# Top-k attention and a routed MoE on one core: one scores tile of two PSUM banks for each head, transposed tails beside the scores of a later unit, and the first q and k pairs loaded in the order of the rest

## The chip, the cores and the metric

One Trainium2 chip, one core of it. The metric is the device time of one launch in microseconds (us); a run of the kernel before takes 391.32 us in the median of three.

## What is computed

Attention over 2 batches, 8 heads, 576 positions of 64 columns, in which each query keeps its 32 largest scores; its rows (1152 tokens of 512 columns) go through a top-1 router to 8 experts of 512 x 1024 x 512.

```python
scores = scale * np.matmul(q, k.transpose(0, 1, 3, 2))
kth = np.partition(scores, -32, axis=-1)[..., -32:-31]
scores = np.where(scores >= kth, scores, -1e9)
attn = np.exp(scores - scores.max(-1, keepdims=True)); attn /= attn.sum(-1, keepdims=True) + 1e-9
x = np.matmul(attn, v)                     # -> (1152, 512)
expert = argmax(x @ w_gate); h = np.maximum(disp @ w1, 0); y = h @ w2
out[i] = gate[i] * y[expert[i], pos[i]]
```

## The kernel before, in words

**Units and rounds.** Queries come in 9 tiles of 128 rows, heads in 4 pairs: 36 units `u` of 128 queries and two heads. `attention` (L1028) writes the program out round by round; round `i` works on several units at once, each at another step. In a round's order: `penalty` of unit i-3 (L391), `heads` of unit i (L289), `sign_turn` of unit i-1 (L363), `shift` of unit i (L339), `probs` of unit i-3 (L400), half of `values` of unit i-4 (L424), `scores` of unit i+1 (L272), the other half of `values`, two steps of `select` for unit i-2, `merge` of unit i (L303). Each engine executes its own instructions in the order in which they are written; the framework adds the semaphore waits between engines, tile by tile. `LAG` and the tables `side`, `early`, `late`, `mid`, `act`, `pool`, `end` say in which round the routing of tokens, the loads and splits of weights and the first expert's matmuls are issued.

**One unit.** PE writes the scores of both heads (L281, eight matmuls, sixteen where a tile spans both batches). VectorE (DVE) takes the 8 largest of each 64-column segment straight from PSUM (`MAX8`, L296, 18 of them, with small steps of earlier units filled in between). ScalarE (ACT) copies the rest: `nn` (L340), then `sm`, the scores less their maximum, one instruction for each head (L343), which are the last reads of the scores in PSUM. Then the sign and its count on ACT (L353), a product on GpSimd (POOL, L360), two 576-column `MAX8` on DVE (L384), the small `nk` (L388), and the penalty on ACT (L398). `probs` transposes `sm` and adds the transposed penalty on PE (L415, L416), four blocks of 128 columns for each head, and ACT takes the exponential (L417). The last 64 columns of both heads, the **tail**, go together as a ninth block: transposed in a tile of its own, `pTt` (L406, L407), exponential in L408. `values` multiplies with v (L437, L440).

**PSUM, 8 banks.** `pD` 1, `pV` 1, `pT` 2 (a tile of each in turn), `pTt` 1, and `trio` 3: in attention these three are one tile `pS` in which head 0 has columns 0 to 575 and head 1 columns 576 to 1151; before and after attention they are three single banks, `TAIL_P`.

**The start.** q and k of batch 0 are loaded pair by pair (`load_qk`, L86), split into two 16-bit halves (`split_qk`), transposed on PE (L231, L234) into PSUM and copied to `qk` in SBUF (`take`, L236; L241 on ACT, L243 on DVE). Pairs 0 and 1 are loaded so that a partition holds 6 consecutive positions, 1536 bytes in one piece; after the transpose the copy puts position 6t+r at its place, writing every sixth element. Pairs 2 and 3 are loaded with 96 positions apart, in pieces of 256 bytes, and the copy is straight. Round 0 starts when the copies of pair 0 are done; pair 1 is copied by ACT before `shift` of unit 0. `swap_q` (L207) makes, by DMA, a copy of q with its halves exchanged. `warm` (L1022) issues matmuls whose result nobody reads.

**Small users of `pTt`.** `pick`, `pick_row`, `check`, `count` and `warm(few)` put a small matmul's result there (L933, L960, L979, L996, L1023).

Of the kernel before, what the change touches and what calls it, by code (L numbers as in the profile page):

```python
# [34 lines left out]
def kernel(  # L35
# [35 lines left out]
    def trio(one):  # L71
        if TRIO.get("one") != one:
            trio_end()
            TRIO["one"], TRIO["cm"] = one, tc.tile_pool(name=f"pS{one}", bufs=1, space=bass.MemoryType.PSUM)
            TRIO["pool"] = TRIO["cm"].__enter__()
        if one:
            return TRIO["pool"].tile([128, 3, 512], FT, name="pS", bufs=1)
        return [TRIO["pool"].tile([128, 512], FT, name=f"pS{i}", bufs=1) for i in range(3)]

# [6 lines left out]
    def load_qk(b, p, tag="nat", names="qk"):  # L86
        for name in names:
            src = q if name == "q" else k
            XN[name, b, p] = x = work.tile([PR, 2, R, D], FT, name=name + "nat", tag=tag, bufs=4 if tag == "nat" else 2)
            for j in range(2):  # L90
                nc.sync.dma_start(x[:, j], bass.AP(
                    tensor=src.tensor, offset=src.offset + (b * H + 2 * p + j) * S * D,
                    ap=[[D, PR], [PR * D, R], [1, D]] if b or p > 1 else [[R * D, PR], [D, R], [1, D]]))

# [141 lines left out]
    def take(p, slot, j, pt, eng):  # L236
        o, pt = qk_of(0)[slot][:, 2 * p + j], pt[:, :S]
        if p < 2:
            o, pt = o.rearrange("p (t r) -> p r t", r=R), pt.rearrange("p (r t) -> p r t", r=R)
        if eng is nc.scalar:  # L240
            eng.activation(o, pt, AF.Copy)  # L241
        else:
            eng.tensor_copy(o, pt)  # L243
# [28 lines left out]
    def scores(u):  # L272
        t, p = divmod(u, HP)

        PS[u] = trio(1).rearrange("p g c -> p (g c)")
        for j in range(2):
            h = 2 * p + j
            for c0, c1 in ((0, 512), (512, S)) if j == 0 else ((0, 1024 - S), (1024 - S, S)):
                for row, n, b, s in parts(t):
                    for i in range(2):  # L280
                        nc.tensor.matmul(PS[u][row:row + n, j * S + c0:j * S + c1], QK[b][2 * i][:, h, s:s + n],  # L281
                                         QK[b][1][:, h, c0:c1], start=(i == 0), stop=(i == 1))

    def scores_of(u, j):
        return PS[u][:, j * S:(j + 1) * S]

# [112 lines left out]

    def probs(u, j):  # L400
        sm = SM[u].rearrange("p j s -> p (j s)")
        pen = PEN[u].rearrange("p j s -> p (j s)")
        if j == 2:
            PTT[u] = work.tile([128, 128], FT, name="pTt")
            pt = psum.tile([128, 128], FT, name="pTt", bufs=1)
            nc.tensor.matmul(pt, sm[:, 512:640], ident, start=True, stop=False, is_transpose=True)  # L406
            nc.tensor.matmul(pt, pen[:, 512:640], identb, start=False, stop=True)  # L407
            nc.scalar.activation(PTT[u], pt, AF.Exp, scale=-scale)  # L408
            return
# [520 lines left out]
    def pick(e, step):  # L930
        if step == 0:
            PK[e] = (psum.tile([128, 128], FT, name="pTt", bufs=1), CG[:, e])
        pc, g = PK[e] if e < 2 else (PKR[1][0], CG[:, 3])  # L933
# [24 lines left out]
    def pick_row(e, step):  # L958
        if step == 0:
            PKR[e] = (psum.tile([128, 128], FT, name="pTt", bufs=1), CG[:, 2 * e])  # L960
            nc.tensor.matmul(PKR[e][0][:1, :E], onesb[:, 0:1], OHS, start=True, stop=True)
# [15 lines left out]
    def check(step):  # L977
        if step == 1:
            pf = psum.tile([128, 128], FT, name="pTt", bufs=1)  # L979
            nc.tensor.matmul(pf[:1, 0:1], onesb[:, 0:1], fl[:, 0:1], start=True, stop=True)  # L980
# [14 lines left out]
    def count():  # L995
        pc = psum.tile([128, 128], FT, name="pTt", bufs=1)  # L996
        nc.tensor.matmul(pc[:1, :E], onesb[:, 0:1], OHS, start=True, stop=True)
# [24 lines left out]
    def warm(n, few=False):  # L1022
        o = psum.tile([128, 128], FT, name="pTt", bufs=1) if few else TAIL_P[2]  # L1023
        x = onesb if few else onesb[:, None, :].to_broadcast([128, 4, 128])
# [3 lines left out]
    def attention(side, early, late, mid, act, pool, end):  # L1028
        nc.vector.memset(OHS, 0.0)
        def run(fs):  # L1030
            for f, *a in fs:
                f(*a)
# [3 lines left out]
        for i in range(NU - 1):  # L1036
# [27 lines left out]
            last = i == NU - 2  # L1064
            exps = at(3, probs, 0) + at(3, probs, 1) + at(3, probs, 2)
            run(exps + at(0, shift) if last else at(0, shift) + exps)
            run(routes((1, 1.5)))
            half, nxt = at(4, values, 1), at(-1, scores)
            run(at(4, values, 0) + (half + nxt if last else nxt + half) + routes((0, 3, 3.5)))
            run(mid.get(i, []) + at(2, select, 1) + at(2, select, 2))  # L1070
# [146 lines left out]
    split_qk(0, 1, 0, POOL, DVE, 2)  # L1217
    pt = [psum.tile([128, 1024], HF, name=f, bufs=n) for f, n in (("pT", 2), ("pT", 2), ("pTt", 1))]
    pt += [a.bitcast(HF) for a in TAIL_P[:2]] + [pv.bitcast(HF)]
    for i, j, sw, o, eng in ((0, 0, 0, 0, ACT), (0, 1, 0, 1, ACT), (0, 0, 2, 3, DVE), (1, 0, 0, 4, ACT),  # L1220
# [137 lines left out]
```

## Time and profile before

| | |
|---|---|
| median of 3 runs | 391.32 us (389.61 to 392.37) |
| profiled execution: its time | 391.26 us |
| its span, first to last instruction | 389.5 us |
| DVE busy | 325.0 us (83%) |
| PE busy | 329.7 us (85%) |
| ACT busy | 303.2 us (78%) |
| POOL busy | 273.9 us (70%) |

The span is what the profile resolves; 1.8 us of the profiled execution's time lie around it. The program has a start (to about 40 us), 36 rounds of some 6.2 us, their end (to about 285 us), and the remaining experts. Busy shares are means over these stages. A PE matmul's length is modelled, and PE's clock has two levels, 1.2 and 2.4 GHz; the profile shows the granted one as 0.50 and 1.00. Line numbers are those of the kernel before; in the changed kernel L281 is L277, L296 is L292, L340 and L343 are L336 and L339, L241 is L237, and L398 is L394, while L406 to L440 keep their numbers.

### The profile page before, as it was taken

The numbers are of one execution on the slowest core, as the hardware profiler recorded it, in microseconds if no ns is written. First come the engines' busy times: TensorE is split into PE (matmuls) and PEld (weight loads), VectorE is DVE, ScalarE is ACT, GpSimd is POOL, SyncE is SP. The second block draws the span as 40 slices with busy tenths as digits, with TensorE's granted clock in tenths as the row PEclk, the third lists the DMA queues.
The fourth block names the chain that finished last, engine by engine and source line by source line (L and its number), as shares of the span: only waits on it lengthen the run. The fifth ranks groups of instructions, "written<-read, shape, count | busy, mean of one in ns | idle before, by whom it ended". The sixth has DMA issues, their size and how long they took to land.

```text
span 389.5 us, 10253 instructions
## 1 busy us (share of the span) xinstructions
PE 329.7 (85%) x3387; PEld 276.0 (71%) x3390; DVE 325.0 (83%) x1863; ACT 303.2 (78%) x573; POOL 273.9 (70%) x293
## 2 busy tenths in 40 slices
PE   5556588789889887978898999999989999899791
PEld 2245477677768776867677888999746996897681
DVE  5747999998998999999999998989791669969920
ACT  6978899998898899989897999796553767768610
POOL 4366595889695678998977989976631459579541
PEclk9556999996997999999988999999999999999997
DMA  8132989794738150304032302557459999999210
GB/s 191 25 91 57 200 199 222 203 236 91 108 65 270 40 206 31 109 3 136 2 109 57 110 2 66 138 164 265 186 102 383 314 317 350 331 333 372 56 31 24
DMA packets 66085, 60.28 MB, mean 155 GB/s; under 512 B 47461, under 2 KB 48229, under 8 KB 66023
## 3 DMA queue, kind: packets, MB, share of 16 engines
q1 hardware_dynamic: 63879, 54.79, 51.3%
q0 software_dynamic: 1616, 4.73, 3.3%
q8 instruction: 28, 0.46, 0.5%
q14 instruction: 34, 0.28, 0.2%
q10 hardware_dynamic: 528, 0.02, 0.1%
HBM read 40.66 MB, written 12.09 MB: 135 GB/s over the span
## 4 chain that ended last, share of the span: by engine, by line
PE 47%; DVE 36%; ACT 10%; issue 3%; DMA 2%; SPq 0%; POOL 0%; ACTq 0%; POOLq 0%
DVE un L296 14%; PE pS L281 7%; PE pV L440 7%; DVE z L384 6%; PE pS L656 6%; PE pT L656 5%; ACT qk L241 4%; PE pT L415 4%; PE pT L738 3%; DVE ws L618 3%; PE pV L656 2%; PE pD L656 2%; PE pT L416 2%; ACT ws L612 2%; DVE wk L319 1%
## 5 line engine op out<-in xcount | busy, mean ns | idle before, releaser
L296 DVE MAX8 un<-pS 128x8 f32<-128x64 f32 x648 | 110.4, 219 | 14.8 <-PE pS L281 14.0
L360 POOL TENSOR_TENSOR z<-sm,sg 128x576 f32<-128x576 f32 x71 | 89.6, 1280 | 21.3 <-ACT sg L353 21.0
L618 POOL TENSOR_TENSOR ws<-wr,ws 128x1024 bf16<-128x1024 f32 x29 | 66.5, 2298 | 18.2 <-ACT ws L612 17.2
L440 PE MATMUL pV<-vm,pT 128*128 128x65 f32 (+1 forms) x640 | 76.9, 270 | 0.0
L281 PE MATMUL pS<-qk 128*128 128x512 f16 (+7 forms) x320 | 47.9, 311 | 33.2 <-DVE na L313 15.5
L656 PEld LDWEIGHTS <-ws 128*128 128x128 f16 (+1 forms) x1056 | 70.3, 98 | 6.6 <-issue 4.7
L440 PEld LDWEIGHTS pV<-vm,pT 128*128 128x128 f32 (+1 forms) x640 | 73.2, 188 | 0.8
L281 PEld LDWEIGHTS <-qk 128*128 128x128 f16 (+1 forms) x320 | 26.3, 109 | 54.5 <-issue 39.2
L618 DVE TENSOR_TENSOR ws<-wr,ws 128x1024 bf16<-128x1024 f32 x35 | 60.7, 1766 | 2.7 <-ACT ws L612 2.2
L415 PE MATMUL pT<-ident,sm 128*128 128x128 f32 x288 | 58.5, 292 | 0.5 <-ACT xT L505 0.5
L353 ACT ACTIVATE sg<-sm,mx 128x576 bf16<-128x576 f32 x72 | 55.0, 767 | 3.2 <-DVE mx L336 2.8
L398 ACT ACTIVATE pen<-sm,nk 128x576 bf16<-128x576 f32 x70 | 50.7, 773 | 6.7 <-DVE nk L388 6.5
L416 PE MATMUL pT<-identb,pen 128*128 128x128 bf16 x288 | 54.7, 227 | 1.0 <-ACT pen L398 0.9
L384 DVE MAX8 z<-z 128x8 f32<-128x576 f32 x72 | 50.8, 747 | 0.0
L612 ACT ACTIVATE ws<-wr 128x1024 f16<-128x1024 f32 x50 | 49.8, 1047 | 0.1
L343 ACT ACTIVATE sm<-pS,mx 128x576 f32<-128x576 f32 x72 | 49.3, 736 | 0.6 <-issue 0.3
L415 PEld LDWEIGHTS pT<-ident,sm 128*128 128x128 f32 x288 | 43.0, 149 | 5.7 <-ACT xT L505 1.6
L417 ACT ACTIVATE pT<-pT 128x512 f32<-128x512 f32 x72 | 39.4, 600 | 2.7 <-PE pT L416 2.5
L661 POOL DMA_INDIRECT out_dram<-y,xp x12 | 17.5, 1462 | 27.7 <-ACT y L803 14.0
L416 PEld LDWEIGHTS <-pen 128*128 128x128 bf16 x288 | 31.1, 109 | 2.1 <-ACT pen L398 1.9
L656 PE MATMUL pS<-xe,ws 128*128 128x128 f16 (+7 forms) x312 | 22.0, 227 | 0.6 <-DVE ws L618 0.6
L542 POOL DMA_INDIRECT xbuf<-xs,ru x9 | 10.1, 1118 | 16.5 <-DVE xs L537 6.5
(257 smaller groups left out, 652.1 us busy)
## 6 DMA issues: line engine op xcount, KB each, us to landing
wr<-in_moe_w_dram SPq DMA_DIRECT2D x32, 1024.0 KB, 6.0
xbuf<-zero SPq DMA_DIRECT2D x6, 771.0 KB, 6.1
qnat<-in_q_dram SPq DMA_DIRECT2D x16, 144.0 KB, 3.5
knat<-in_k_dram SPq DMA_DIRECT2D x16, 144.0 KB, 3.5
out_dram<-zero SPq DMA_DIRECT2D x3, 768.0 KB, 4.6
vm<-in_v_dram SPq DMA_DIRECT2D x16, 128.0 KB, 3.0
qk<-qk SPq DMA_DIRECT2D x14, 144.0 KB, 2.5
vt<-in_v_dram SPq DMA_DIRECT2D x4, 64.0 KB, 3.2
```

What stands on the lines that cost most here:

```text
L281: nc.tensor.matmul(PS[u][row:row + n, j * S + c0:j * S + c1], QK[b][2 * i][:, h, s:s + n], QK[b][1][:, h, c0:c1], start=(i == 0), stop=(i ...
L296: nc.vector.max(out=un[:, j, i], in_=scores_of(u, j)[:, i * w:(i + 1) * w])
L353: nc.scalar.activation(SG[u][j], SM[u][:, j], AF.Sign, bias=VAL[u][0][:, 2, j:j + 1], scale=-(1.0 - 2.0 ** -20), accum_out=CNT[:, c:c + 1])
L360: engs[j].tensor_tensor(out=Z[u][:, j], in0=SM[u][:, j], in1=SG[u][j], op=OP.mult)
L384: nc.vector.max(out=z8[:, step - 1], in_=Z[u][:, step - 1])
L398: nc.scalar.activation(PEN[u][:, j], SM[u][:, j], AF.Relu, bias=NK[u][:, j:j + 1], scale=BIG)
L415: nc.tensor.matmul(pt[:, c], sm[:, o:o + 128], ident, start=True, stop=False, is_transpose=True)
L416: nc.tensor.matmul(pt[:, c], pen[:, o:o + 128], identb, start=False, stop=True)
L440: nc.tensor.matmul(PV[t][row:row + n, h0 + half], PT[u][:, half, c, row:row + n], VM[b][:, c, p, half], start=False, stop=(half == 1 and c ...
L612: nc.scalar.activation(h[:, d], r[:, s], AF.Copy)
L618: eng.tensor_tensor(out=l[:, d], in0=r[:, s], in1=h[:, d], op=OP.subtract)
L656: nc.tensor.matmul(o, a(i), c(i), start=(i == 0 and m == 0), stop=(i == k - 1 and m == 2))
```

## The change

Head 0 and head 1 of a unit get a tile of two banks each (`pS0`, `pS1`), four banks in all; the fourth is that of `pTt`, which is gone. The transposed tail of unit i-3 is written into columns 640 to 767 of head 1's tile of unit i+1, after that unit's scores and before the second half of `values`. For the last four units it takes a fourth single bank or, for unit 32, a tile `pT`. The small users of `pTt` take a tile `pT`. Pairs 0 and 1 of q and k of batch 0 are loaded as the others are, and their copies are straight.

```diff
         if one:
-            return TRIO["pool"].tile([128, 3, 512], FT, name="pS", bufs=1)
-        return [TRIO["pool"].tile([128, 512], FT, name=f"pS{i}", bufs=1) for i in range(3)]
+        return [TRIO["pool"].tile([128, 1024 if one else 512], FT, name=f"pS{i}", bufs=1) for i in range(2 if one else 4)]
...
-                    ap=[[D, PR], [PR * D, R], [1, D]] if b or p > 1 else [[R * D, PR], [D, R], [1, D]]))
+                    ap=[[D, PR], [PR * D, R], [1, D]]))
...
-        if p < 2:
-            o, pt = o.rearrange("p (t r) -> p r t", r=R), pt.rearrange("p (r t) -> p r t", r=R)
...
-            for c0, c1 in ((0, 512), (512, S)) if j == 0 else ((0, 1024 - S), (1024 - S, S)):
+            for c0, c1 in ((0, 512), (512, S)):
...
-                        nc.tensor.matmul(PS[u][row:row + n, j * S + c0:j * S + c1], QK[b][2 * i][:, h, s:s + n],
+                        nc.tensor.matmul(PS[u][j][row:row + n, c0:c1], QK[b][2 * i][:, h, s:s + n],
...
-    def probs(u, j):
+    def probs(u, j, later=None):
...
-            pt = psum.tile([128, 128], FT, name="pTt", bufs=1)
+            if later is not None:
+                pt = PS[later][1][:, 640:768]
+            else:
+                pt = TAIL_P[3][:, :128] if TAIL_P else psum.tile([128, 128], FT, name="pT", bufs=2)
...
-            PKR[e] = (psum.tile([128, 128], FT, name="pTt", bufs=1), CG[:, 2 * e])
+            PKR[e] = (psum.tile([128, 128], FT, name="pT", bufs=2), CG[:, 2 * e])
...
-            exps = at(3, probs, 0) + at(3, probs, 1) + at(3, probs, 2)
+            exps = at(3, probs, 0) + at(3, probs, 1)
...
-            run(at(4, values, 0) + (half + nxt if last else nxt + half) + routes((0, 3, 3.5)))
+            run(at(4, values, 0) + (half + nxt if last else nxt + at(3, probs, 2, i + 1) + half))
+            run((at(3, probs, 2, i + 1) if last else []) + routes((0, 3, 3.5)))
```

On PE, in a round of the middle (`pT` and `sm`, `pen` are the transposed block and its two sources, `pV` the product with v, `pS` the scores), before: the tail stands ahead of `values` and of the scores, and the first matmul of the scores waits for the one tile.

```order
L406 MATMUL pTt_1653<-ident_102,sm_1249 128x128
L407 LDWEIGHTS pen_1581
L407 MATMUL pTt_1653<-identb_104,pen_1581 128x128
L437 MATMUL pV_127<-vt0_70,pTt_1537 128x130 [waits DVE_49]
L440 MATMUL pV_127<-vm0_69,pT_1516 128x65 x4
L281 LDWEIGHTS qk_192 [waits DVE_49,PE_49]
L281 MATMUL pS_1662<-qk_193,qk_192 128x512 [waits Activation_49]
```

The same round now, from the last matmul of head 0 on: head 1's first matmul has a wait of its own, and the tail (L406, L407) follows it into the same tile.

```order
L277 MATMUL pS0_1661<-qk_193,qk_194 128x64
L277 LDWEIGHTS qk_192 [waits DVE_49,PE_49]
L277 MATMUL pS1_1662<-qk_193,qk_192 128x512 [waits Activation_49]
L277 LDWEIGHTS qk_194
L277 MATMUL pS1_1662<-qk_193,qk_194 128x512
L277 LDWEIGHTS qk_192
L277 MATMUL pS1_1662<-qk_193,qk_192 128x64
L277 LDWEIGHTS qk_194
L277 MATMUL pS1_1662<-qk_193,qk_194 128x64
L406 MATMUL pS1_1662<-ident_102,sm_1253 128x128
L407 LDWEIGHTS pen_1585
L407 MATMUL pS1_1662<-identb_104,pen_1585 128x128
```

The tail's two matmuls have moved from ahead of half of `values` to behind all of the scores.

On DVE, the `heads` of a middle unit now (`un` receives the segments' maxima, `pS0` and `pS1` are the two heads' scores):

```order
L377 TENSOR_TENSOR pD_119<-pD_119,CNT_125 128x16 [waits DVE_49]
L292 MAX un_2081<-pS0_2039 128x8 x4
L292 MAX un_2081<-pS1_2040 128x8 [waits Activation_49]
L533 SCALAR_TENSOR_TENSOR r4_1806,r5_1807<-pV_127,oh_1809 128x8 [waits PE_49,Pool_49]
L292 MAX un_2081<-pS1_2040 128x8 x8
```

In the kernel before, only a unit's first `MAX` waits (for PE); now head 1's first one waits for ACT, whose last access to that tile is the exponential of the tail (L408).

On PE in round 34, before, where `probs` of unit 31 follows the first expert's matmuls (L738) and `pick_row` holds its small tile:

```order
L738 MATMUL pT_4610<-ws1_3291,hl_4075 128x128
L415 MATMUL pT_4714<-ident_102,sm_4233 128x128 [waits PE_49]
L416 LDWEIGHTS pen_4635 [waits Activation_49]
L416 MATMUL pT_4714<-identb_104,pen_4635 128x128
L415 MATMUL pT_4714<-ident_102,sm_4233 128x128
```

And now:

```order
L738 MATMUL pT_4614<-ws1_3295,hl_4079 128x128
L415 MATMUL pT_4718<-ident_102,sm_4237 128x128 [waits Activation_49]
L416 LDWEIGHTS pen_4639
L416 MATMUL pT_4718<-identb_104,pen_4639 128x128
L415 MATMUL pT_4718<-ident_102,sm_4237 128x128
```

The first block waits for ACT's read of L738's tile, and head 1's first block for ACT's exponential of head 0's (before: for ACT's read of L738's tile), because `pick_row` holds one of the two `pT` banks there.

## Rows read from the trace of the kernel before

**Rows 1.** The profile's first page: the span, then the busy time of each engine (us, share of the span, instructions), and the granted TensorE clock in 40 equal slices of the span, in tenths of full speed (a 9 stands for 90% or more).

```profile
span 389.5 us, 10253 instructions
PE 329.7 (85%) x3387; PEld 276.0 (71%) x3390; DVE 325.0 (83%) x1863; ACT 303.2 (78%) x573; POOL 273.9 (70%) x293
...
PEclk9556999996997999999988999999999999999997
```

**Rows 2.** Busy time by stage, two stretches: start and end, length, then busy us and instructions of PE, PEld, DVE, ACT and POOL, then the granted clock, the DMA share and GB/s.

```profile
42.00:212.00 170.00, 142.49 (x1298) 119.95 (x1299) 163.09 (x1244) 151.59 (x327) 137.76 (x152) 0.93 0.51 127
212.00:257.00 45.00, 44.28 (x496) 40.06 (x497) 42.50 (x321) 40.96 (x94) 42.32 (x52) 1.00 0.28 85
```

**Rows 3.** Who waited for whom (total us, times, longest), DVE in 42 to 212 us, DVE in 212 to 257 us, and PE in 212 to 257 us.

```profile
DVE un L296 <- PE pS L281: 6.6, 12, 1.1
...
DVE un L296 <- PE pS L281: 2.2, 2, 1.3
...
PE pS L281 <- DVE vb L309: 0.7, 2, 0.5
```

**Rows 4.** Instructions in order of time around one hand-over from unit to unit, 153 to 157 us: start, length of the merged piece, engine, line, operation, out<-in, count, and in brackets the idle time before it and what ended that.

```profile
153.71 1.37 ACT L343 ACTIVATE sm<-pS,mx 128x576 f32<-128x576 f32 x2 [0.29 <-issue]
...
154.97 1.08 ACT L417 ACTIVATE pT<-pT 128x512 f32<-128x512 f32 x2
...
155.13 1.14 PE L281 MATMUL pS<-qk 128*128 128x512 f16 x8 [1.53 <-ACT sm L343]
...
155.93 0.30 ACT L408 ACTIVATE pTt<-pTt 128x128 f32<-128x128 f32 x1
156.19 1.45 ACT L398 ACTIVATE pen<-sm,nk 128x576 bf16<-128x576 f32 x2
...
156.31 0.23 DVE L296 MAX8 un<-pS 128x8 f32<-128x64 f32 x1 [0.15 <-PE pS L281]
```

**Rows 5.** Instructions in order of time, the program's first 40 us (rows of ACT, DVE and PE, the same columns).

```profile
6.51 4.04 ACT L241 ACTIVATE qk<-pT 128x576 f16<-128x576 f16 x2
...
8.21 1.57 DVE L205 SCALAR_TENSOR_TENSOR hl<-qnat,hl 96x768 f16<-96x768 f32 x1 [0.73 <-POOL hl L201]
9.70 2.07 DVE L243 COPY qk<-pS 128x576 f16<-128x576 f16 x1
...
11.48 2.22 DVE L243 COPY qk<-pTt 128x576 f16<-128x576 f16 x1
...
13.40 1.08 DVE L205 SCALAR_TENSOR_TENSOR hl<-knat,hl 96x768 f16<-96x768 f32 x1
14.02 8.01 ACT L241 ACTIVATE qk<-pT 128x576 f16<-128x576 f16 x4
...
15.31 2.46 DVE L296 MAX8 un<-pS 128x8 f32<-128x64 f32 x18 [0.81 <-issue]
...
16.35 0.64 PE L231 MATMUL pT<-identh,hl 96*128 96x96 f16 x6 [1.14 <-ACT qk L241]
...
21.66 1.01 ACT L199 ACTIVATE hl<-knat 96x768 f16<-96x768 f32 x1
...
22.57 0.24 ACT L340 ACTIVATE nn<-un 128x72 f32<-128x72 f32 x1
22.72 1.35 ACT L343 ACTIVATE sm<-pS,mx 128x576 f32<-128x576 f32 x2
...
24.12 2.08 PE L281 MATMUL pS<-qk 128*128 128x512 f16 x8 [1.40 <-DVE na L323]
...
26.24 0.23 DVE L296 MAX8 un<-pS 128x8 f32<-128x64 f32 x1 [2.05 <-PE pS L281]
...
33.31 1.19 ACT L241 ACTIVATE qk<-pT 128x576 f16<-128x576 f16 x2 [1.14 <-PE pT L231]
...
40.04 0.23 DVE L296 MAX8 un<-pS 128x8 f32<-128x64 f32 x1 [0.96 <-PE pS L281]
```

**Rows 6.** One line's instructions: the copies of line 241 out of a tile pT (count, then shortest, median and longest in ns, first and last start), and the one DVE copy of 512 columns from PSUM in line 503.

```profile
L241 ACT ACTIVATE qk<-pT x14: 642/651/2315, 6.5 to 35.2; 128x576 f16<-128x576 f16 x14
...
L503 DVE COPY xT<-pS x1: 682/682/682, 260.1 to 260.1; 128x512 f32<-128x512 f32 x1
```

**Rows 7.** Time from issue to landing of the loads of line 91: those issued before 1.5 us (rows of 1536 bytes), those issued at 4.9 to 6 us (rows of 256 bytes, behind five pairs of loads), those issued at 19.5 and 20.1 us (rows of 256 bytes, alone); then busy time by stage with the DMA share and GB/s at the end, 2 to 6 us (rows of 1536 bytes) and 77 to 79 us (rows of 256 bytes).

```profile
DMA to landing us min/median/max: 2.9/2.9/2.9
...
DMA to landing us min/median/max: 4.4/4.5/4.6
...
DMA to landing us min/median/max: 2.8/2.8/2.8
...
2.00:6.00 4.00, 3.08 (x7) 0.94 (x7) 2.69 (x14) 1.89 (x4) 0.76 (x17) 1.00 0.97 253
...
77.00:79.00 2.00, 1.84 (x20) 1.55 (x19) 2.00 (x18) 2.00 (x4) 0.00 (x0) 1.00 0.94 218
```

**Rows 8.** Stretches in which the granted clock was 0.50 after 46 us: the sum row of five of them (46.8 to 50.2, 87.8 to 94.6, 115.1 to 121.9, 193.6 to 197, 207.2 to 210.7 us), and one wait of DVE behind the third.

```profile
sum 23.90, PE 23.61 PEld 18.31 DVE 21.06 ACT 21.10 POOL 22.56; mean PE 4.72 PEld 3.66 DVE 4.21 ACT 4.22 POOL 4.51
...
124.00 0.23 DVE L296 MAX8 un<-pS 128x8 f32<-128x64 f32 x1 [1.15 <-PE pS L281]
```

**Rows 9.** The last rounds, in order of time: PE's transposes of unit 32's tail, and ACT's exponentials before it (two instructions in one piece).

```profile
254.16 0.28 PE L406 MATMUL pTt<-ident,sm 128*128 128x128 f32 x1
...
253.84 1.12 ACT L417 ACTIVATE pT<-pT 128x512 f32<-128x512 f32 x2
```

More of the change, by code (lines that the diff above doesn't have):

```diff
@@ L75, in trio @@
             TRIO["pool"] = TRIO["cm"].__enter__()
-        if one:
-            return TRIO["pool"].tile([128, 3, 512], FT, name="pS", bufs=1)
-        return [TRIO["pool"].tile([128, 512], FT, name=f"pS{i}", bufs=1) for i in range(3)]
+        return [TRIO["pool"].tile([128, 1024 if one else 512], FT, name=f"pS{i}", bufs=1) for i in range(2 if one else 4)]
     ctx.enter_context(tc.manual_schedule())
@@ L273, in scores @@
         t, p = divmod(u, HP)
-        PS[u] = trio(1).rearrange("p g c -> p (g c)")
+        PS[u] = trio(1)
         for j in range(2):
             h = 2 * p + j
-            for c0, c1 in ((0, 512), (512, S)) if j == 0 else ((0, 1024 - S), (1024 - S, S)):
+            for c0, c1 in ((0, 512), (512, S)):
                 for row, n, b, s in parts(t):
                     for i in range(2):
-                        nc.tensor.matmul(PS[u][row:row + n, j * S + c0:j * S + c1], QK[b][2 * i][:, h, s:s + n],
+                        nc.tensor.matmul(PS[u][j][row:row + n, c0:c1], QK[b][2 * i][:, h, s:s + n],
                                          QK[b][1][:, h, c0:c1], start=(i == 0), stop=(i == 1))
     def scores_of(u, j):
-        return PS[u][:, j * S:(j + 1) * S]
+        return PS[u][j][:, :S]
     def heads(u, fill):
@@ L931, in pick @@
         if step == 0:
-            PK[e] = (psum.tile([128, 128], FT, name="pTt", bufs=1), CG[:, e])
+            PK[e] = (psum.tile([128, 128], FT, name="pT", bufs=2), CG[:, e])
         pc, g = PK[e] if e < 2 else (PKR[1][0], CG[:, 3])
@@ L978, in check @@
         if step == 1:
-            pf = psum.tile([128, 128], FT, name="pTt", bufs=1)
+            pf = psum.tile([128, 128], FT, name="pT", bufs=2)
             nc.tensor.matmul(pf[:1, 0:1], onesb[:, 0:1], fl[:, 0:1], start=True, stop=True)
@@ L995, in count @@
     def count():
-        pc = psum.tile([128, 128], FT, name="pTt", bufs=1)
+        pc = psum.tile([128, 128], FT, name="pT", bufs=2)
         nc.tensor.matmul(pc[:1, :E], onesb[:, 0:1], OHS, start=True, stop=True)
@@ L1022, in warm @@
     def warm(n, few=False):
-        o = psum.tile([128, 128], FT, name="pTt", bufs=1) if few else TAIL_P[2]
+        o = psum.tile([128, 128], FT, name="pT", bufs=2) if few else TAIL_P[2]
         x = onesb if few else onesb[:, None, :].to_broadcast([128, 4, 128])
@@ L1217 @@
     split_qk(0, 1, 0, POOL, DVE, 2)
-    pt = [psum.tile([128, 1024], HF, name=f, bufs=n) for f, n in (("pT", 2), ("pT", 2), ("pTt", 1))]
-    pt += [a.bitcast(HF) for a in TAIL_P[:2]] + [pv.bitcast(HF)]
+    pt = [psum.tile([128, 1024], HF, name="pT", bufs=2) for i in range(2)]
+    pt += [a.bitcast(HF) for a in (TAIL_P[3], TAIL_P[0], TAIL_P[1], pv)]
     for i, j, sw, o, eng in ((0, 0, 0, 0, ACT), (0, 1, 0, 1, ACT), (0, 0, 2, 3, DVE), (1, 0, 0, 4, ACT),
```

## The prediction

> **What bounds the kernel now.** I read the page first: VectorE (DVE), TensorE (PE) and ScalarE (ACT) are each busy for about four fifths of the 389.5 us, none for all of it [rows 1]. So the stages have to be read apart. By stage, from 42 to 212 us DVE is busy 163.09 of 170 us, ACT 151.59, PE 142.49; from 212 to 257 us, where the first expert's matmuls are mixed in, PE is busy 44.28 of 45 us [rows 2]. In the first stretch DVE is the bound, less 6.91 us of idle time; who ends that idle time is a question for the waits: 6.6 us in 12 waits of `heads` for the scores of PE, the longest 1.1 [rows 3]. The hand-over shows why: the scores (1.14 us for two heads) start when ACT has ended both `sm` (153.71 + 1.37 = 155.08), though head 0's was ready after half of them, and `heads` starts at 156.31, when all scores of both heads are there [rows 4]. ACT runs on for both exponentials, the tail and two penalties meanwhile.
>
> The first 40 us read otherwise. There the copies out of PSUM stand in a row: two ACT copies take 4.04 us, four take 8.01, two DVE copies 2.07 and 2.22, while two straight ones of pair 2 take 1.19 at 33.31 [rows 5]; of line 241's 14 copies the median is 651 ns and the longest 2315 [rows 6]. The slow ones write every sixth element. DVE's first `heads` begins at 15.31, its second only at 26.24, behind a wait of 2.05 us for PE [rows 5].
>
> **The start: the strided copies go.** ACT has eight of them in a row: two of pair 0 at 6.51, pair 0's other two up to 14.02, and pair 1's four (q, then k) up to 14.02 + 8.01 = 22.03 [rows 5]. Straight, each is 0.65 [rows 6]. DVE's two, of pair 0, stand behind a split that ends at 8.21 + 1.57 = 9.78 and take 2.07 and 2.22 [rows 5]; straight I put each at 0.68, by the nearest row, a DVE copy of 512 columns from PSUM in 682 ns [rows 6]. They then end at 11.1 and are the last of pair 0. Head 0's scores take 1.04 us (half of the 2.08 in the row at 24.12, at half clock), so `heads` of unit 0 starts at about 12.4 in place of 15.31 and, 2.46 long, is no longer in the way. Head 1's scores end at 13.4; behind them PE transposes pair 1's k (0.64 us, twice), and ACT's last copy ends at 13.4 + 1.28 + 0.65 and a hand-over, 15.5. A split of 1.01 (the row at 21.66) follows, and ACT comes to `nn` at 16.4 in place of 22.57. `sm` of head 0 ends at about 17.25, the next scores' first half takes 1.04, and `heads` of unit 1 starts at 18.3 in place of 26.24: 7.9 us sooner [rows 5]. Units 2 and 3 follow by the same chain, with pair 2's copies, already straight, in it (33.31): for unit 3, at 40.04 before, I come to 31.5, 8.5 sooner [rows 5]. Less 0.3 for loads that land later, that is **-8.2 us**. Lower bound: only pair 1's four count, 8.01 - 4 x 0.60 = 5.6. Upper bound: all eight, 15.52 - 8 x 0.65 = 10.3.
>
> **The loads get smaller pieces.** Eight loads change from pieces of 1536 to 256 bytes, 1.18 MB. By latency the rows differ little: 2.9 us from issue to landing for large pieces, 2.8 for small ones alone, 4.4 to 4.6 for small ones behind a crowd. By rate: 253 GB/s with queues 0.97 busy, against 218 at 0.94 where small pieces flow [rows 7]. At 218 the same bytes take 5.4 us and not 4.66, so the last of them comes 0.75 later and the first hardly later; 0.2 to 0.75, inside the 8.2. The Trainium skill, "DMA: Bandwidth & Descriptors", section "Specifications", asks for transfers of at least 512 bytes for line rate, and its section "Why small descriptors are slow (HBM only)" works out 11 cycles for 256 bytes where 8 carry data. That speaks against the change; by that rule the rate falls by 27%, and 4.66 us become 6.4, which would make the sum 380.1. The trace agrees in direction, with 14% (218 of 253) and no later landing of a load alone.
>
> **The middle: the scores in two tiles.** Two things come sooner. Head 0's scores wait only for the first `sm`, 0.68 us before the end of the second (half of 1.37), and DVE can begin when half of the matmuls are done, 0.57 us (half of 1.14) [rows 4]. Together 1.25 us; and the tail's matmuls no longer stand ahead of the scores. DVE's waits here are 6.6 us in 12, at most 1.15 us (the one at 124.00) [rows 3, 8]. So all of them fit into 1.25 but for what PE has from elsewhere (about 0.4 us, in the wait at 124.00, where the clock was low). That leaves 6.2 recovered; all of DVE's idle time would be 6.91. ACT has 18.4 us of idle time in this stretch and PE 27.5 [rows 2], so neither binds by its sum, but each waits for the other within a round; I take 1.0 of that back for it and set **-5.2 us**, with bounds 0 (what DVE gains it waits for ACT's `sm` or penalty in the next round) and -6.9.
>
> From 212 to 257 us PE is full [rows 2]. DVE's 2.2 us of waits [rows 3] are PE's own lateness and nothing there is won by starting a head earlier, except where PE itself stands waiting: 0.7 us for DVE [rows 3]. **-0.7 us**, bounds 0 and -2.2.
>
> **What the change adds.** The tail's exponential (0.30 us [rows 4]) keeps its place in ACT's queue, but PE now issues the tail behind the scores of head 1, and these wait for the second `sm`. In the hand-over: 155.08 + 0.57 for head 1 + 0.28 for the tail [rows 9] and a hand-over each way, about 156.1; ACT comes to the tail when its two exponentials end, 154.97 + 1.08 = 156.05 [rows 4]. So ACT waits some 0.1 us at full clock; at half clock the PE work doubles and ACT waits about 1.0. Behind it in ACT's queue stand the penalties, and behind those PE's `probs` of the next round and `sm`. Head 1's first `MAX8` must wait for that exponential too, as both use one tile; but it is due only after head 0's nine, 9 x 0.23 = 2.1 us or more behind the start of `heads` at about 155.3, so at 157.4, where the exponential ends at 156.4: 1 us of cover (at half clock 157.3 and 158.0, 0.7 us).
>
> In round 34 `pick_row` holds one of two `pT` banks, and `probs` of unit 31 is forced through the other: head 1's block waits for the exponential of head 0's. An exponential is 0.56 (half of 1.12 [rows 9]), and with the hand-over to PE and four transposes behind it ACT and PE take turns: about 1.0 us, in a stage where PE has none to spare. In round 35 the tail of unit 32 is a third `pT` tile: it waits for the first of two exponentials, 253.84 + 0.56 = 254.40 against 254.16 [rows 9], and what follows waits for the second: about 0.5. Together **+1.5 us**, bounds 0.3 (only the 0.24 in sight) and 2.5. The experts' fourth single bank saves nothing where PE is full: 0.
>
> **Sum.** -8.2 - 5.2 - 0.7 + 1.5 = -12.6 on a span of 389.5 us. The profiled execution took 391.26 us, 1.8 around its span; its 391.26 is 0.06 from the median of the runs, so no correction: 391.3 - 12.6 = **378.7 us**. By the bounds: -10.3 - 6.9 - 2.2 + 0.3 = -19.1 at best (372.2), -5.6 - 0 - 0 + 2.5 = -3.1 at worst (388.2). I do not think that all ends fall together, so the range is 373.0 to 386.5.
>
> **Rivals.** *Only the start is repaid* (chance 0.20). DVE's idle time goes back to ACT: at a hand-over ACT works from 153.71 to 157.64 without a gap [rows 4], so a round that begins sooner finds the penalty or `sm` just as late. For it: ACT is at 151.59 of 170. Against it: ACT's idle time is 18.4 us, DVE's 6.9. Then -8.2 + 1.5 = -6.7: 384.6 us.
>
> *The small pieces hold the start up* (0.09). The first pairs land 1.6 us later, as 4.5 against 2.9 us allow [rows 7], and pair 1's, at the end of the same queue, by as much again. Then the start gives 8.2 - 3.2 = 5.0: 381.9 us. Against it: these slow landings stand behind five pairs of other loads.
>
> *Slower: the tail's wait on ACT lengthens every round* (0.05). Place: between the exponentials and the penalty. Price: 170 / 6.2 = 27 rounds; if ACT waits w in each, its 151.59 becomes 151.59 + 27w. It binds above w = 0.68 and cancels the whole gain (8.2 less 1.5) above w = (18.4 + 6.7) / 27 = 0.93. At w = 1.25 the middle takes 185.3 us: 170 + 15.3, and the kernel 391.3 + 15.3 - 6.7 = 400 us. For it: at half clock w is about 1.0. Against it: after 46 us only 23.9 us run at 0.50 [rows 8], and at full clock w is 0.1. It needs a kernel that loses its clock through most rounds; the page has it at 9 or more in most slices after the first four [rows 1].
>
> **How the numbers follow.** Forecast 0.66, and the three rivals 0.20, 0.09 and 0.05; I give the range 8 in 10 and leave out the last and the far ends of the others. About 1% (3.9 us) is what a measurement of this kernel can tell from no change. The forecast's case lies wholly beyond that; of the first rival, with the start at its lower bound of 5.6 the gain is 4.1, so a quarter of it ends within 1%. With two in a hundred for a forecast that misses altogether: faster 0.88, same 0.07, slower 0.05.
>
> **What would show each step.** Right: all copies of the old line 241 near 650 ns; `heads` of unit 1 near 18.3 and of unit 3 near 31.8 us; DVE's waits for the scores between 32 and 200 us down from 6.6 to about 1.5 us; ACT's idle time before the tail's exponential about 0.1 us; idle time before the last rounds' transposes up by 1 to 2 us. Wrong: unit 1 at 20 or later with a wait for a load or a split (second rival); DVE's waits that are gone for PE but are there for ACT's penalty or its `nk`, POOL's product or `sm` (first rival); ACT's wait at the tail above 0.7 us in most rounds, or a granted clock of 0.50 for much more than 24 us after 40 us (third).

## The result and the profile after

The changed kernel takes **375.29 us** in the median of four runs (374.97 to 377.30); the kernel before 390.47 in four. The ratio is 0.962, 95% interval 0.956 to 0.969. The forecast was 378.7 us, range 373.0 to 386.5: right in direction and in range, 3.4 us below the forecast. Ratios here and below leave out executions more than 1.5% above the fastest of the same kernel; medians keep them all. The profiled execution of the changed kernel has a span of 373.4 us, 16.1 less than [rows 1] where 12.6 were forecast.

Where it came from is read best from one landmark that both programs have: the first `MAX8` of each unit's `heads` on DVE. In us, from the two traces:

| from | to | before | after | difference | forecast |
|---|---|---|---|---|---|
| start of the span | unit 4 | 45.87 | 35.02 | -10.85 | -8.2 |
| unit 4 | unit 29 | 163.38 | 156.01 | -7.37 | -5.2 |
| unit 29 | unit 33 | 25.76 | 25.50 | -0.26 | -0.7 |
| unit 33 | first product with unit 32's tail (L437) | 20.80 | 22.57 | +1.77 | +1.5 |
| there | end of the span | 133.7 | 134.3 | +0.6 | 0 |

First the page of the changed kernel (busy us and share, then the granted clock in 40 slices), to be read against [rows 1]:

```profile
span 373.4 us, 10232 instructions
PE 326.8 (88%) x3390; PEld 269.4 (72%) x3390; DVE 321.1 (86%) x1863; ACT 291.9 (78%) x573; POOL 273.2 (73%) x293
...
PEclk9778999999999999999989999999999999999897
```

But for the copies, which are shorter, the work is the same; the gaps are shorter. The slices at half clock after the start are fewer too, which comes back below. The start, ACT and DVE in order of time, against [rows 5]:

```profile
4.70 0.84 ACT L197 ACTIVATE hl<-qnat 96x768 f16<-96x768 f32 x1 [1.99 <-DMA qnat<-in_q_dram]
...
7.05 1.19 ACT L237 ACTIVATE qk<-pT 128x576 f16<-128x576 f16 x2
...
9.69 0.81 DVE L239 COPY qk<-pS 128x576 f16<-128x576 f16 x2
12.02 2.46 DVE L292 MAX8 un<-pS 128x8 f32<-128x64 f32 x18 [0.56 <-ACT qk L237]
...
13.38 1.19 ACT L237 ACTIVATE qk<-pT 128x576 f16<-128x576 f16 x2 [1.67 <-PE pT L229]
14.46 0.84 ACT L197 ACTIVATE hl<-knat 96x768 f16<-96x768 f32 x1
15.20 0.26 ACT L336 ACTIVATE nn<-un 128x72 f32<-128x72 f32 x1
...
16.85 0.23 DVE L292 MAX8 un<-pS 128x8 f32<-128x64 f32 x1
...
21.87 0.23 DVE L292 MAX8 un<-pS 128x8 f32<-128x64 f32 x1 [0.46 <-PE pS L277]
```

Unit 1 starts at 16.85 (forecast 18.3, before 26.24); the copies of pair 0 are down from 4.04 to 1.19 for two, and DVE's two take 0.81 together. ACT now waits for PE (1.67 us) where PE waited for ACT.

The middle, units 4 to 29 of the changed kernel, first as a stage (columns as in [rows 2]):

```profile
35.00:191.00 156.00, 134.77 (x1263) 110.67 (x1264) 155.50 (x1195) 145.43 (x315) 133.12 (x150) 0.99 0.50 133
```

And the waits there (total us, times, longest), all that the answer has for DVE, and of ACT's the one at the tail:

```profile
DVE rs L451 <- PE pV L440: 0.3, 1, 0.3
...
ACT pTt L408 <- PE pS L407: 1.8, 5, 0.6
```

DVE is busy for 155.50 of 156.00 us: its waits for the scores [rows 3] are gone, but for one of 0.24 us at the very end, when unit 29 starts at 191.03. ACT waits for the tail 1.8 us in all, not in every round. The hand-over that answers to [rows 4]:

```profile
137.27 1.37 ACT L339 ACTIVATE sm<-pS,mx 128x576 f32<-128x576 f32 x2
...
138.06 1.28 PE L277 MATMUL pS<-qk 128*128 128x512 f16 x8 [0.73 <-ACT sm L339]
...
139.58 0.28 ACT L408 ACTIVATE pTt<-pS 128x128 f32<-128x128 f32 x1
...
139.97 0.22 DVE L292 MAX8 un<-pS 128x8 f32<-128x64 f32 x1
```

PE starts 0.79 us behind the start of the two `sm`, in the middle of them, and has written all scores (139.34) before DVE comes for the first.

### The profile page after: what moved, and what is told of

Its sections match the earlier page's. It is cut to its first block, busy times and chain, and to the rows that moved or that the text cites. A ratio compares the mean times of both kernels' runs of the same rounds, so it can differ in the third digit from the quotient of the medians.

```text
span 373.4 us, 10232 instructions
## 1 busy us (share of the span) xinstructions
PE 326.8 (88%) x3390; PEld 269.4 (72%) x3390; DVE 321.1 (86%) x1863; ACT 291.9 (78%) x573; POOL 273.2 (73%) x293
## 4 chain that ended last, share of the span: by engine, by line
DVE 50%; PE 36%; ACT 5%; issue 4%; DMA 2%; POOL 1%; SPq 1%; POOLq 0%; ACTq 0%
DVE un L292 17%; DVE z L380 10%; PE pS L656 8%; PE pV L440 5%; PE pT L656 4%; PE pD L656 3%; DVE ws L618 3%; DVE wk L315 2%; DVE wk L312 2%; PE pS L277 2%; PE pT L415 2%; PE pT L738 2%; ACT ws L612 2%; DVE vb L317 2%; DVE na L309 1%
## 5 line engine op out<-in xcount | busy, mean ns | idle before, releaser
L656 PEld LDWEIGHTS <-ws 128*128 128x128 f16 (+1 forms) x1056 | 71.8, 99 | 6.5 <-issue 4.7
L440 PE MATMUL pV<-vm,pT 128*128 128x65 f32 (+1 forms) x640 | 74.2, 264 | 0.0
L440 PEld LDWEIGHTS pV<-vm,pT 128*128 128x128 f32 (+1 forms) x640 | 70.4, 183 | 0.9 <-issue 0.6
L277 PE MATMUL pS<-qk 128*128 128x512 f16 (+3 forms) x320 | 47.3, 297 | 14.7 <-ACT sm L339 14.7
L416 PE MATMUL pT<-identb,pen 128*128 128x128 bf16 x288 | 53.1, 223 | 5.6 <-ACT pen L394 5.5
L277 PEld LDWEIGHTS <-qk 128*128 128x128 f16 (+1 forms) x320 | 27.2, 107 | 37.2 <-issue 20.2
L415 PEld LDWEIGHTS pT<-ident,sm 128*128 128x128 f32 x288 | 41.7, 145 | 11.0 <-ACT xT L505 2.9
L416 PEld LDWEIGHTS <-pen 128*128 128x128 bf16 x288 | 29.9, 106 | 9.8 <-ACT pen L394 9.7
L656 PE MATMUL pS<-xe,ws 128*128 128x128 f16 (+2 forms) x336 | 22.8, 226 | 0.0
```

The costliest lines, as they stand in the source:

```text
L277: nc.tensor.matmul(PS[u][j][row:row + n, c0:c1], QK[b][2 * i][:, h, s:s + n], QK[b][1][:, h, c0:c1], start=(i == 0), stop=(i == 1))
L415: nc.tensor.matmul(pt[:, c], sm[:, o:o + 128], ident, start=True, stop=False, is_transpose=True)
L416: nc.tensor.matmul(pt[:, c], pen[:, o:o + 128], identb, start=False, stop=True)
L440: nc.tensor.matmul(PV[t][row:row + n, h0 + half], PT[u][:, half, c, row:row + n], VM[b][:, c, p, half], start=False, stop=(half == 1 and c ...
L656: nc.tensor.matmul(o, a(i), c(i), start=(i == 0 and m == 0), stop=(i == k - 1 and m == 2))
```

## Experiments

Times of `heads` are from the profiled execution of each kernel. "Unit 4" is when unit 4 starts, "the middle" is from unit 4 to unit 29.

### The two halves of the change by themselves

`start_only` is the kernel before with the changed `load_qk` and `take`; `tiles_only` is the changed kernel with the old ones.

```diff
-                    ap=[[D, PR], [PR * D, R], [1, D]] if b or p > 1 else [[R * D, PR], [D, R], [1, D]]))
+                    ap=[[D, PR], [PR * D, R], [1, D]]))
...
-        if p < 2:
-            o, pt = o.rearrange("p (t r) -> p r t", r=R), pt.rearrange("p (r t) -> p r t", r=R)
```

> The kernel before with only the loads of pairs 0 and 1 and their copies changed; tiles and tail as before. Parts add up: unit 4's heads at about 35.0 us as in the changed kernel (45.9 before), DVE's waits for the scores in the middle still about 6.6 us, so 390.5 - 10.9 = about 379.6 us. Rival, the clock: the early start alone keeps the clock up and the middle gains too, waits under 3 us, about 375.5. Rival, paid back: a later load or split holds the middle up, 384 or more.

> The changed kernel with the old loads and strided copies of pairs 0 and 1. Parts add up: unit 4 at 45.9 us as before, 7.4 us won from unit 4 to unit 29, 0.4 to unit 35, then 1.9 to 2.5 given back: 390.5 - 5.5 = about 385 us. Rival: the middle's gain needs the early start (its clock, or loads that are out of the way), then 389 to 391.

`start_only`: 383.48 us (380.58 to 387.42), ratio 0.986 (0.978 to 0.994); unit 4 at 38.74, the middle 159.40. `tiles_only`: 382.49 us (380.76 to 383.69), ratio 0.981 (0.974 to 0.988); unit 4 at 42.35, the middle 155.81. So at unit 4 the loads and copies give 7.13 us and the tiles 3.52, together 10.65 of the 10.85 measured. My expectation put the whole 10.9 on the copies: wrong, the tiles win a third of the start. The shares hold to about 1 us: three kernels with the old start and the one tile have unit 4 at 45.87, 46.81 and 46.92, four with the new start and the new hand-over between 34.15 and 35.32. At units 1 to 4 DVE waits for the scores 2.18, 1.18, 0.96 and 0.81 us in `start_only`, with the one tile; with two, in the changed kernel, it waits once, 0.46 us at unit 2 (the row at 21.87 above). The first of `start_only`'s waits:

```profile
19.38 0.23 DVE L294 MAX8 un<-pS 128x8 f32<-128x64 f32 x1 [2.18 <-PE pS L279]
```

The ratios agree with the sum: 0.986 times 0.981 is 0.967, and both together measured 0.962. In the middle `tiles_only` has all of the gain, and `start_only`, which should have had none, has 4.0 of it. DVE's waits for the scores there are 3.9 us (5.9 in the same units before), and the stage reads:

```profile
38.70:198.10 159.40, 135.03 (x1272) 114.19 (x1271) 155.95 (x1193) 144.81 (x315) 132.74 (x149) 0.96 0.49 128
```

The granted clock of that stretch is 0.96, and 0.93 in the kernel before [rows 2]. Hence the next question.

### Is half of the middle's gain the clock?

`before_warm` is the kernel before with ten small matmuls ahead of the scores, in the rounds where PE stands waiting; they add zeros to the product of `values`.

```diff
+        zeros = consts.tile([128, 128], BF)
+        nc.vector.memset(zeros, 0.0)
+
+        def busy(u, n):
+            h0 = 2 * (u % 2)
+            for i in range(n):
+                nc.tensor.matmul(pv[:, h0 * (D + 1):h0 * (D + 1) + 128], zeros, onesb, start=False, stop=False)
...
-            run(at(4, values, 0) + (half + nxt if last else nxt + half) + routes((0, 3, 3.5)))
+            run(at(4, values, 0) + (half + nxt if last else ([(busy, i - 4, 10)] if 5 < i < 29 else []) + nxt + half) + routes((0, 3, 3.5)))
```

> The kernel before with ten small matmuls that add zeros to the running product, ahead of the scores of rounds 6 to 28, where PE stands waiting; tiles, tail and start as before. Theory: half of the middle's gain is the clock that fell behind PE's waits and made the next hand-overs later; with PE busier the clock stays up after 55 us (before: 20 us at 0.50 between 55 and 211 us), DVE's waits fall from 5.9 to 3 us, and unit 4 to unit 29 takes 159 to 160.5 us in place of 163.4. Rival: the clock is not the cause, or the added matmuls make the scores later by themselves: 163 or more.

The middle takes 159.89 us instead of 163.38, and after 51 us the clock is full until 361 us. The stage, then DVE's waits in it:

```profile
46.90:206.80 159.90, 144.10 (x1502) 123.49 (x1501) 155.74 (x1193) 144.80 (x315) 132.35 (x149) 0.99 0.48 128
```

```profile
DVE un L296 <- PE pS L281: 4.7, 6, 1.2
```

DVE's waits fell only to 4.7, not to 3: the added matmuls stand ahead of the scores where a hand-over is tight (0.84 us at units 10, 14 and 26, where it was about 0.29). The time of the whole is 388.97 us (386.67 to 391.86), ratio 0.998 (0.994 to 1.002): on the median nothing clear is won. The trace shows what was asked, though: the one-tile hand-over takes 159.4 to 160.2 us for the middle at a clock of 0.96 to 0.99 (this kernel, `start_only`, and `tail_moved` below), and 163.4 at 0.93; the two-tile one 155.8 to 156.0 at 0.99 to 1.00. So of the 7.4 us, 3.4 to 4.4 are left when the clocks are alike. The waits of the kernel before divide in the same sense. Of its 5.9 us in units 5 to 28, five waits with 1.6 us stand at full clock (units 10, 14, 21, 22 and 26), and six with 4.25 us stand inside a stretch at half clock or up to 2.3 us behind one. Here are units 10, 11 and 12, around the stretch from 87.8 to 94.6 us:

```profile
82.60 0.23 DVE L296 MAX8 un<-pS 128x8 f32<-128x64 f32 x1 [0.29 <-PE pS L281]
...
90.10 0.23 DVE L296 MAX8 un<-pS 128x8 f32<-128x64 f32 x1 [0.82 <-PE pS L281]
...
96.88 0.23 DVE L296 MAX8 un<-pS 128x8 f32<-128x64 f32 x1 [0.70 <-PE pS L281]
```

`start_only` has the same five waits at full clock, 1.6 us, and 2.3 us in four others at or just behind half clock. From these two traces I estimate that at full clock throughout the one tile would cost DVE some 1.6 us of waits in these units. Most of what the two tiles win in the middle of the traced execution is thus lateness at half clock that no longer reaches DVE, or half clock that did not occur.

Whether the change itself keeps the clock up stays open. After 55 us and before 340 us the clock is at half for 20.5, 10.2 and 3.4 us in the traces of the kernel before, `start_only` and `tail_moved`, and for 0 or 3.4 in all traces with two tiles; but `both_heads` below, with the new hand-over undone, has 0 too. The profiled execution of the kernel before lies low: its mean granted clock is 0.928, that of 46 others on record 0.919 to 0.973 with a median of 0.940. Most of the whole gain is not the clock: the five of those 46 with 0.958 or more take 386.0 to 391.4 us, the four of the changed kernel, with 0.961 to 0.970, 375.0 to 377.3.

### Which part of the hand-over?

In the changed kernel two orders can be turned around: which head's `sm` ACT makes first, and which head's scores PE writes first. `both_heads` turns the scores alone (PE waits for both `sm`, and DVE, which begins with head 0, for all scores, as before the change); `late_pe` turns `sm` alone (PE late, DVE needs half); `early_pe` turns both (PE early, DVE needs all).

```diff
     def scores(u):
...
-        for j in range(2):
+        for j in (1, 0):
...
     def shift(u):
...
-        for j in range(2):
+        for j in (1, 0):
```

> The changed kernel, but PE writes head 1's scores first and head 0's behind them, so that, as in the kernel before, the scores wait for both sm and DVE waits for all of the scores; tiles, tail and start stay. Theory, the hand-over: DVE's waits come back, 4 to 6.6 us between unit 4 and unit 29, about 381 us. Rival, the tail's new place (PE no longer has it ahead of the scores) or the clock of the early start makes the middle's gain: waits under 2 us, 376.5 us or less.

> The changed kernel with ACT making sm of head 1 first, so that head 0's scores wait for the second sm (0.68 us later) while DVE still needs only half of the matmuls. With both halves of the hand-over undone (the run both_heads) 5.1 us of 7.4 between unit 4 and unit 29 were lost. Theory, a threshold: what is late is hidden until it exceeds DVE's cover, so one half alone costs little: 156.0 us before become 156 to 157.5, DVE waits under 1.5 us. Rival, each part pays by its size: 0.68 of 1.25, 2.8 us lost, 158.8.

> The changed kernel with head 1 ahead of head 0 in ACT's sm and in PE's scores, so that PE starts after the first sm, but DVE, which begins with head 0, waits for all of the scores (0.57 us later). Theory, a threshold: 156 to 157.5 us from unit 4 to unit 29 (156.0 in the changed kernel), DVE waits under 1.5 us. Rival, each part pays by its size: 0.57 of 1.25, 2.3 us lost, 158.3.

| | PE after | DVE needs | time (us) | ratio to before | unit 4 | middle | clock there |
|---|---|---|---|---|---|---|---|
| changed kernel | first `sm` | half | 375.29 | 0.962 (0.956 to 0.969) | 35.02 | 156.01 | 0.99 |
| `early_pe` | first `sm` | all | 376.87 | 0.962 (0.956 to 0.968) | 37.53 | 157.34 | 0.98 |
| `late_pe` | second `sm` | half | 379.12 | 0.969 (0.962 to 0.976) | 35.95 | 158.52 | 0.99 |
| `both_heads` | second `sm` | all | 387.88 | 0.991 (0.986 to 0.995) | 39.94 | 161.14 | 0.98 |

With both undone the middle loses 5.1 us and the start 4.9. The theory of the hand-over holds; the rival, that the tail's new place or the early start make the gain, falls. `both_heads` came out far above the 381 us expected, in part since I had thought of the middle alone and the start adds its 4.9. DVE's waits for the scores in the middle of `both_heads`, then those of `early_pe`, and the longest of these, just behind a stretch at half clock (36.4 to 43.2 us):

```profile
DVE un L292 <- PE pS L277: 5.0, 8, 1.9
```

```profile
DVE un L292 <- PE pS L277: 1.4, 2, 1.0
```

```profile
44.43 0.23 DVE L292 MAX8 un<-pS 128x8 f32<-128x64 f32 x1 [0.98 <-PE pS L277]
```

So DVE's half matters mostly where the clock is low: 2.5 us at unit 4, and 1.4 in the middle in two waits, the other one of 0.40 at full clock. My threshold holds for it. For PE's early start it does not: `late_pe` loses 2.5 in the middle, near the rival's 2.8, without one wait at `heads`. PE is late for what follows, and DVE meets it at the product of `values`: 1.5 us more than in the changed kernel. Another 0.8 us is busy time of DVE, 156.25 against 155.50, whose cause is open. The waits of DVE, then of PE, which is 12.0 us in 18 in the changed kernel:

```profile
DVE rs L451 <- PE pV L440: 1.8, 7, 0.3
...
PE pS L277 <- ACT sm L339: 21.2, 19, 1.5
```

The expectations left out a wait that comes with PE's lateness. The tail stands behind the scores, so ACT has to wait for it in all 25 rounds of the middle, first in `both_heads`, then in `late_pe`:

```profile
ACT pTt L408 <- PE pS L407: 14.9, 25, 2.2
```

```profile
ACT pTt L408 <- PE pS L407: 12.4, 25, 0.7
```

The kernel before, with its tail ahead of the scores, has no such wait in the middle, so `both_heads` is not quite its hand-over. `tail_moved`, below, has the wait (12.8 us in 25) with the one tile, and its middle is at most 0.8 us longer than that of `start_only` and `before_warm`: half a microsecond in a round is below the 0.68 at which the prediction has ACT bind. The 5.1 us are thus mainly the hand-over, and up to about 1 us of them (161.14 against 160.20) is not assigned.

### The tail's place, and the small pieces

`tail_moved` is the kernel before with the tail's transposes behind the scores, in their own bank. `large_q` is the changed kernel with q of pairs 0 and 1 in the old large pieces.

```diff
-            exps = at(3, probs, 0) + at(3, probs, 1) + at(3, probs, 2)
+            exps = at(3, probs, 0) + at(3, probs, 1)
...
-            run(at(4, values, 0) + (half + nxt if last else nxt + half) + routes((0, 3, 3.5)))
+            run(at(4, values, 0) + (half + nxt if last else nxt + at(3, probs, 2) + half))
+            run((at(3, probs, 2) if last else []) + routes((0, 3, 3.5)))
```

```diff
-                    ap=[[D, PR], [PR * D, R], [1, D]]))
+                    ap=[[R * D, PR], [D, R], [1, D]] if name == "q" and not b and p < 2 else [[D, PR], [PR * D, R], [1, D]]))
```

> The kernel before with only the tail's transposes moved behind the scores, in its own bank as before. Theory: PE waits for sm ahead of the scores anyway (1.53 us in the hand-over shown), so the tail ahead of them costs nothing: 163.4 us from unit 4 to unit 29, within 1 us but for differences of the clock, total as before. Rival: the tail stood in the way of the scores and its move gives 2 us or more of the middle's 7.4.

> The changed kernel with q of pairs 0 and 1 loaded in pieces of 1536 bytes, k in 256; the copies stay straight, so that the queries of these heads stand in another order and the output is another, at the same work. Theory: the first q is on ACT 0.5 us sooner (4.16 instead of 4.70), but the start is held by copies and transposes, and unit 1 begins at most 0.5 us before 16.85. Rival: the small pieces cost the start 1.6 us or more, and unit 1 begins at 15.3 or sooner.

`tail_moved`: 391.02 us, ratio 1.002 (0.997 to 1.007), unit 4 at 46.81. Its middle of 160.20 at a clock of 0.98 is that of the one-tile hand-over, with ACT waiting for the tail:

```profile
ACT pTt L408 <- PE pTt L407: 12.8, 25, 1.5
```

Moving the tail wins nothing by itself; what it does is free a bank. `large_q`, whose queries stand in another order: one execution, 374.07 us. ACT's first split starts at 4.34 us (4.70 with small pieces) and unit 1 at 16.70 (16.85): 0.36 us at the load, 0.15 at unit 1. Unit 4 starts at 34.23, 0.79 sooner, but `end_order` below, with small pieces, has it at 34.15. The rival of 1.6 us falls for q; k was not tried in large pieces.

### The time given back at the end

Three kernels move the small tiles that take a `pT` bank in rounds 33 to 35. `end_free` puts `pick_row` into columns 640 to 767 of head 0's tile of unit 34 and unit 32's tail into head 1's of unit 35. `end_tail` only puts that tail ahead of its eight other blocks. `end_order` does that, and puts `pick_row` into head 1's tile of unit 34:

```diff
-            PKR[e] = (psum.tile([128, 128], FT, name="pT", bufs=2), CG[:, 2 * e])
+            PKR[e] = (PS[34][1][:, 768:896] if e else psum.tile([128, 128], FT, name="pT", bufs=2), CG[:, 2 * e])
...
-        seq(probs, L - 3, steps=(0, 1, 2))
+        seq(probs, L - 3, steps=(2, 0, 1))
```

> The changed kernel with pick_row of round 33 in the free columns of head 0's tile of unit 34 and unit 32's tail in those of head 1's tile of unit 35, so that neither takes one of two pT banks. Theory: the 1.9 us given back between unit 35 and the first full expert go for 1.5 to 1.9 of it: 373.5 us. Rival: PE is full there and the waits were covered: 375.0 or more.

> The changed kernel with unit 32's tail ahead of its eight other blocks, and nothing else. Theory: the waits of 0.1 and 0.30 us go, 0.4 us at most; rounds 33 and 34 as in the changed kernel. Rival: the tail in front makes the first block's exponential 0.3 us later, and nothing is won.

> The changed kernel with pick_row of round 33 in the free columns of head 1's tile of unit 34 (DVE comes to that tile 2 us later than to head 0's) and unit 32's tail ahead of its eight other blocks, in the pT ring. Theory: PE's four waits there (0.46, 0.69, 0.1 and 0.30 us) go and DVE gets none in their place: 1.0 to 1.5 us less from unit 33 to the first full expert, about 374.0 us. Rival: something else is late there all the same, within 0.4 us of the changed kernel, 375.

The waits in question, PE of the changed kernel:

```profile
226.63 0.33 PE L415 MATMUL pT<-ident,sm 128*128 128x128 f32 x1 [0.46 <-ACT y L707]
...
228.22 0.33 PE L415 MATMUL pT<-ident,sm 128*128 128x128 f32 x1 [0.69 <-ACT pT L417]
...
237.76 1.05 PE L738 MATMUL pT<-ws,hh 128*128 128x128 f16 x16 [0.30 <-ACT pT L417]
```

In `end_free` the first two are gone from PE, and DVE has two longer ones in their place:

```profile
223.91 0.23 DVE L292 MAX8 un<-pS 128x8 f32<-128x64 f32 x1 [1.98 <-PE pS L961]
...
236.78 0.76 DVE L292 MAX8 un<-pS 128x8 f32<-128x64 f32 x5 [1.06 <-ACT pTt L408]
```

`heads` waits for a matmul and an exponential in the same tile, though in other columns. From unit 33 to the first product with unit 32's tail it takes 22.75 us: nothing won, the expectation missed. Five of its six runs took 374.02 to 375.18 us and one 1742.86 us; the cause of that one is not known, so it is no version to use. `end_tail`: 375.01 us (372.66 to 377.14), ratio 0.962 (0.957 to 0.967). Its time shows no gain, as the rival had it; in its trace the wait of 0.30 us is gone, and the stretch takes 22.05 us, 0.5 less. In `end_order` head 1's tile is met 2 us later, and DVE does not wait for `pick_row`; the second row ends the stretch:

```profile
221.31 0.23 DVE L292 MAX8 un<-pS 128x8 f32<-128x64 f32 x1 [0.34 <-PE pS L277]
```

```profile
235.68 0.44 PE L437 MATMUL pV<-vt,pTt 128*128 128x130 f32 x2
```

The same stretch takes 20.93 us (235.68 - 214.75) where the changed kernel needs 22.57, so the 1.77 us given back return, but for 0.1: about 0.5 by the tail's order and 1.1 by `pick_row`'s place. It takes **372.95 us** (371.40 to 376.12), ratio to before 0.958 (0.952 to 0.964): the shortest of all, 2.3 us below the changed kernel by medians that were not taken side by side, with intervals that overlap. Its traced span is 3.1 us shorter, of which this stretch explains 1.6.

## Why the prediction was right

**The start** was forecast at -8.2 us and measured -10.85, beyond its bound of 10.3. The mechanism was right: copies out of the row, PE then ACT as the chain. The sizes were off. Of the 2.65 us missed, 1.45 are there at unit 1 (16.85 against 18.3) and the rest by unit 3 (29.20 against 31.8). To unit 1, DVE's straight copy takes 0.44 us (two in 0.81) and not the 0.68 of a copy of 512 fp32 columns, my nearest row; it moves 16-bit values. The Trainium skill, "VectorE: DVE Perf Modes", section "What auto-detection actually checks", has the engine take a double-rate mode where every tensor is 16-bit with step 1; the trace agrees as far as 444 ns for 576 16-bit columns against 682 ns for 512 fp32 ones goes, and shows the step of 6 at 2.07 to 2.22 us. And ACT came to `nn` at 15.20 and not 16.4, since PE's transposes of pair 1's k ended at 13.60 and not at 13.4 + 1.28:

```profile
12.70 0.90 PE L229 MATMUL pT<-identh,hl 96*128 96x96 f16 x12
```

They take 0.90 us and not 1.28, in part because the granted clock is at full again from 13.2 us, where I had reckoned with half. How much is luck of this execution is open: three other traces with the new start and the new hand-over have unit 1 between 15.77 and 17.53, all sooner than 18.3. Units 2 and 3 were carried along "by the same chain", from unit 1 to unit 3 in 13.2 us; it took 12.35. What I left out there are DVE's waits of 0.8 to 2.2 us with the one tile (`start_only`), at half clock for units 1 and 4 (scores of 2.08 us), at full clock for 2 and 3 (1.14 us). The two tiles take 3.5 us out of the start by `tiles_only`; I had counted them for units 0 and 1 alone.

**The middle** was forecast at -5.2 and measured -7.37; DVE has almost no idle time left, the end that I called the bound; the gain goes 0.5 beyond that bound of 6.9, since DVE's busy time fell as well, from 156.5 to 155.5 us, a term that the forecast did not have. The 1.25 us of the hand-over (0.68 for PE, 0.57 for DVE) covers the waits as worked out. The 1.0 us that I took back for ACT and PE did not have to be: ACT ran with less idle time [rows 2] and no new wait on DVE appeared. The size also holds a part that the forecast did not separate, the waits at and behind half clock, 4.25 of 5.9 us. I had them in the 6.6 us as waits like others.

**From unit 29** -0.26 against -0.7; the changed kernel's trace is at half clock just ahead of it, from 187.3 to 190.7 us, and the traces of `tiles_only`, `end_free` and `end_order`, at full clock, take 24.8 us where it takes 25.5. **The added waits** +1.77 against +1.5, at the places named (round 34: 0.46 and 0.69; round 35: 0.30), and `end_order` confirms them by their removal. The last 134 us were forecast unchanged and took 0.6 more, in an execution with the clock at half from 347.7 to 351.1 us. No experiment was made on it; `tiles_only`, `early_pe`, `late_pe`, `end_free` and `large_q`, without that stretch, take 133.1 to 134.4, so that 0.6 is no more than the traces differ by.

**The rivals.** *Only the start is repaid* falls by the middle's 7.37. *Small pieces* falls, by 4.70 against 4.16 us at ACT's first split in the two traces, 0.54 us, and by `large_q`. *The tail's wait on ACT* needed more than 0.93 us in every round and has 1.8 us in five waits; its place was right, as `late_pe` and `tail_moved` show, where it does come in every round, with 12.4 and 12.8 us in 25.

**The range.** The two large terms both fell beyond their own bounds (10.85 against 10.3, 7.37 against 6.9). Those bounds were too narrow. The smaller terms gave 1.3 us less than forecast; had they come out as forecast, the sum would be 373.9, near the end of the range.

## What to carry to other kernels

Split a PSUM tile at the point where its reader and its writer change over: the writer starts one reader's instruction sooner, and the reader needs half of the writer's work. Which of the two pays depends on what is slower at that place: here mostly the writer's early start at full clock, the reader's half at half clock. When a tile is shared for want of space, put the guest into the tile that is met last: the program's waits go by tiles, so its users wait for one another whatever columns they touch. And read a wait apart by the granted clock before pricing it: what is worth 4 us in one execution may be worth less in another.

## What the runs showed of the hardware

Copies of 576 16-bit columns from PSUM: with each sixth element written 2.0 to 2.3 us on ACT and 2.07 to 2.22 on DVE, straight 0.65 and 0.44. Loads in pieces of 256 bytes instead of 1536 moved the first split by 0.4 to 0.5 us. The scores of one unit took 1.14 us on PE at full clock and 2.08 at half. The hand-over of one tile cost 3 to 4 us more in the middle where the granted clock was 0.93 than where it was 0.96 to 0.99; with two tiles the one stretch at half clock there (187.3 to 190.7 us) left waits of 0.24 and 0.29 us, at units 29 and 30.
